# Banded attention and a feed-forward layer on one core: one search's list of steps for another's, and a common order for the transfers of two engines

## The chip, the cores and the metric

The kernel runs on one core of a Trainium2 chip. The metric is the device time of one execution in microseconds (us); the figure to compare is the median over the timed runs. In the profile, PE is TensorE (matmuls), DVE is VectorE, ACT is ScalarE, POOL is GpSimd and SP is SyncE; "ACTq" and "SPq" are DMA transfers that ACT and SP issue. L1243 is line 1243 of the kernel before.

## The reference

```python
def _attn_ref(q, k, v):                      # (8, 8, 576, 64) each
    scores = scale * np.matmul(q, k.transpose(0, 1, 3, 2))
    mask = (rel >= 0) & (rel < window)       # window 64
    scores = np.where(mask, scores, -1000000000.0)
    scores = scores - np.max(scores, axis=-1, keepdims=True)
    attn = np.exp(scores)
    attn = attn / (np.sum(attn, axis=-1, keepdims=True) + 1e-09)
    return np.matmul(attn, v)
def _moe_ref(x, w_in, w_out):                # x (4608, 512), w_in (512, 2048)
    h = x @ w_in
    g = np.maximum(0.01 * h, h)
    return g @ w_out
```

The attention's output, with the heads side by side, is the feed-forward layer's x. All arrays are float32.

## The kernel before

**Stages.** The 4608 tokens go through the feed-forward layer in nine chunks of 512. Weights and activations are split into a high and a low part, and each product of a weight tile and an activation tile is three matmuls of 128 x 128 by 128 x 512 (high by high, high by low, low by high). The first three chunks are multiplied directly: the steps W of the opening and then `early_first` (h, L1038) and `early_second` (acc, L1047). The other six chunks are taken as three pairs with a seven-product scheme: `product` (m, L1243) for x @ w_in, `seventh` (z, L1309) for g @ w_out. Around a product ACT does `put` (L1249) and `leaky` (L1255) and DVE does `add` (L1252); around `seventh` ACT does `wide_high` (L1286) and DVE `wide_low` (L1290) and `combine` (L1293). The sums of weights that this scheme needs are prepared from weights kept in DRAM: ACT issues `fetch` (L1149) and, when the sum is made, `keep` (L1162 and L1165); POOL issues `fill` (L1227), which brings them back.

**Attention between the products.** There are 36 pairs of attention blocks. Pair m needs `load_qk(m)` (a 512 KB transfer issued by ACT, L262), `scores_of(m)` on PE (s, L369), the mask on DVE (L755) or, for some pairs, `copy_of` on ACT (L761), `max_of` on POOL, `minus_of` on DVE (L777), `exp_of` on ACT (L781), `add_of` on POOL, a few small transfers issued by SP, `values_of(m)` on PE (o, L829) and `product_of` on DVE (L854). So PE alternates between groups of feed-forward matmuls and these short visits, called S(m) and V(m) here.

**The order.** Every engine works off its own instructions in the order in which the kernel is written. That order is a list. In the kernel before, it is in two parts: ORDER holds 514 named steps of the opening (raw0, S0, W3, ...), run one after the other; then `op`, `load` and `bulk` collect 2303 numbered steps with what each comes after, and `arrange` runs them in the order of the list PLACES. The end of the file (L1514) chains each engine's instructions in issue order.

**Transfers and semaphores.** Apart from POOL's 84, the program has 475 transfers, 291 of SP and 184 of ACT. The framework gives each of these one of eight semaphores (LANES = 8) in turn, in the order in which its scheduler sees them. A transfer that has the semaphore of an earlier one is issued when that one has landed; until then its engine stands, with all that is listed behind it. In the program before, the turn of SP's and ACT's transfers is that of the scheduler, and 191 of the 475 have another place in it than in the written order, by up to 17 places.

**Steps by number.** The steps that are spoken of below: 818 is S(23), 843 is S(24), 841 is `load_qk(24)`, 820 is `copy_of(23, 0)`, 1285 is a `put` after the product 1284, 800 is `exp_of(22, 0)`, 1213 and 1214 are two `keep` and 1215 and 1216 two `fetch`; 793 is S(22) with `load_qk(22)` as 791, 492 a leaky ACT step after the product step 487, 778 `copy_of(21, 0)` and 766 `exp_of(20, 0)`; 1104 is S(35) with `load_qk(35)` as 1102, 1737 a `put` and 1063 `exp_of(33, 0)`; 961 is V(26), 1411 an `add`, 1425 and 1429 `wide_low`, 924 and 927 `minus_of(27, ...)`, 1461 a `combine`, 914 `product_of(24)`. At the end 2290, 2296 and 2300 are the last `seventh` steps, 2291, 2297 and 2301 the last three additions on DVE (`add_part`, L1329), and 2292 (of 2291), 2298 (of 2297) and 2302 (of 2301) send these results (`send_part`, L1332); 2270 sends an earlier one.

Of the kernel before, what the change touches and what calls it, by code (L numbers as in the profile page):

```python
# [61 lines left out]
PLACES = """  # L62
# [134 lines left out]
def band_attention_ffn(ctx: ExitStack, tc: tile.TileContext, qk, vW, vL, w_in, w_out, eye_mask, out, outT):  # L197
# [415 lines left out]
    def step(name):  # L613
        kind = name.rstrip("0123456789")
        return partial(acts[kind], int(name[len(kind) :]))

    order, late = ORDER.split("|")
    for name in order.split():
        step(name)()
    prev = jobs[-1]  # L620


    plan = []

# [951 lines left out]
```

## Time and profile before

| what | value |
|---|---|
| timed runs | 838.98, 838.88 and 843.11 us; median 838.98 us |
| profiled execution | span 841.2 us, 2.2 us above that median |
| PE busy | 829.1 us of it (99%), 6733 matmuls |
| DVE, POOL, ACT busy | 630.8, 381.5, 369.7 us |
| DMA | 225.75 MB, mean 268 GB/s |

The span of the profiled execution is from the first to the last instruction or transfer of its trace, and the page shows no time around it. PE is close to always busy; what can be read for a change of order are the few places where it is not, and how near the others are to becoming such places. The views used are the table of windows (busy time of each engine in a stretch), the waits (idle time of an engine by the instruction that it waited before and by what released it), timelines, and the chain of work that ended last.

### The profile page before, as it was taken

The page shows a single profiled execution, that of the slowest core. Times are in us where ns is not written, and L with a number is a line of the kernel's source. Part 1 is how long each engine was busy: PE and PEld are TensorE (multiplying, and loading weights), DVE is VectorE, ACT ScalarE, POOL GpSimd, SP SyncE. Part 2 cuts the span into 40 slices and gives each one's busy share as a digit, 9 for nine tenths or more (in the row PEclk, how much of TensorE's full clock was granted, in tenths as well). Part 3 has the DMA queues.
Part 4 walks back from the last instruction along what each step waited for, and adds up shares of the span by engine and source line. Part 5 has one row for each costly group of instructions (what it writes and reads, how often), then busy time and mean ns, then how long its engine had stood idle before and what let it go on. Part 6 is the DMA issues. An engine that isn't in the chain of part 4 may idle for free.

```text
span 841.2 us, 16743 instructions
## 1 busy us (share of the span) xinstructions
PE 829.1 (99%) x6733; PEld 678.1 (81%) x6733; DVE 630.8 (75%) x912; ACT 369.7 (44%) x599; POOL 381.5 (45%) x216
## 2 busy tenths in 40 slices
PE   8999999999999999989999999999999999999997
PEld 5777888888888888868888888887888888888886
DVE  6999897777766698667888987559799863366773
ACT  4666555344423355243564442233545422325432
POOL 5332000897867747687672116797941111111110
PEclk9999999999999999999999999999999999999999
DMA  9886866987887899999999798899998996677772
GB/s 327 278 276 209 310 223 225 319 287 259 277 295 251 271 342 379 365 299 359 361 321 308 224 316 251 255 282 241 261 278 243 317 257 184 190 197 200 212 200 89
DMA packets 131005, 225.75 MB, mean 268 GB/s; under 512 B 15856, under 2 KB 53744, under 8 KB 130928
## 3 DMA queue, kind: packets, MB, share of 16 engines
q0 software_dynamic: 53568, 88.09, 38.8%
q10 hardware_dynamic: 36608, 78.26, 27.6%
q1 hardware_dynamic: 40752, 58.34, 21.7%
q8 instruction: 53, 0.87, 0.4%
q14 instruction: 24, 0.20, 0.1%
HBM read 167.28 MB, written 57.26 MB: 267 GB/s over the span
## 4 chain that ended last, share of the span: by engine, by line
PE 89%; DMA 5%; DVE 3%; issue 1%; ACT 1%; POOL 0%; DVEq 0%; ACTq 0%
PE z L1309 27%; PE m L1243 25%; PE acc L1047 11%; PE h L1038 11%; PE acc L558 4%; PE s L369 4%; PE h L522 4%; PE o L829 3%; DMA w_sums<-pspare 2%; DMA qk<-qk 1%; DMA raw<-w_in 1%; DMA raw<-w_out 1%; DMA w_single<-w 1%; PE o L458 0%; DVE raw L321 0%
## 5 line engine op out<-in xcount | busy, mean ns | idle before, releaser
L1243 PE MATMUL m<-pfew,p 128*128 128x512 f32 x720 | 171.6, 394 | 3.0 <-ACT pxa L1249 2.5
L1243 PEld LDWEIGHTS m<-pfew,p 128*128 128x128 f32 x720 | 135.5, 189 | 32.5 <-ACT pxa L1249 2.9
L1309 PE MATMUL z<-gs,p 128*128 128x512 f32 (+1 forms) x360 | 86.0, 387 | 0.0
L1047 PE MATMUL acc<-p,gs 128*128 128x512 f32 x324 | 80.7, 393 | 0.0
L1309 PE MATMUL z<-pxa,p 128*128 128x512 f32 x324 | 78.5, 391 | 0.0
L1309 PEld LDWEIGHTS z<-gs,p 128*128 128x128 f32 x360 | 67.3, 188 | 13.9
L1309 PE MATMUL z<-pspare,p 128*128 128x512 f32 x324 | 78.0, 389 | 0.0
L1252 DVE TENSOR_TENSOR pxa<-m,pxa 128x512 f32<-128x512 f32 x60 | 41.2, 688 | 48.5 <-PE m L1243 43.6
L770 POOL PARTITION_ALL_REDUCE g<-late_f x20 | 36.3, 1842 | 86.6 <-DVE late_f L755 71.5
L1227 POOL DMA_DIRECT2D p<-w_first x42 | 31.7, 755 | 93.7 <-PE m L1243 51.6
L1309 PEld LDWEIGHTS z<-pspare,p 128*128 128x128 f32 x324 | 60.7, 188 | 12.6
L1309 PEld LDWEIGHTS z<-pxa,p 128*128 128x128 f32 x324 | 60.5, 188 | 12.9 <-issue 0.2
L1243 PE MATMUL m<-pxb,p 128*128 128x512 f32 x288 | 70.6, 391 | 0.0
L1047 PEld LDWEIGHTS acc<-p,gs 128*128 128x128 f32 x324 | 60.0, 188 | 12.8
L773 POOL PARTITION_ALL_REDUCE late_o<-late_f x20 | 65.2, 3274 | 9.6 <-ACT late_f L781 7.4
L773 POOL PARTITION_ALL_REDUCE late_o<-e x18 | 61.5, 3432 | 16.6 <-issue 7.9
L1252 DVE TENSOR_TENSOR p<-m,pxa 128x512 f32<-128x512 f32 x60 | 40.7, 687 | 36.6 <-PE m L1243 35.9
L773 POOL PARTITION_ALL_REDUCE late_o<-late_e x18 | 59.3, 3321 | 10.6 <-ACT late_e L781 6.0
L1243 PEld LDWEIGHTS m<-pxb,p 128*128 128x128 f32 x288 | 53.8, 188 | 11.4
L1227 POOL DMA_DIRECT2D p<-w_sums x24 | 18.0, 749 | 93.1 <-PE z L1309 76.8
L1038 PE MATMUL h<-pxa,p 128*128 128x512 f32 x228 | 55.9, 392 | 0.0
L1038 PEld LDWEIGHTS h<-pxa,p 128*128 128x128 f32 x228 | 42.4, 188 | 9.0
(201 smaller groups left out, 1600.5 us busy)
## 6 DMA issues: line engine op xcount, KB each, us to landing
p<-w_first POOLq DMA_DIRECT2D x42, 1024.0 KB, 7.0
p<-w_sums POOLq DMA_DIRECT2D x24, 1024.0 KB, 6.7
p<-w_second POOLq DMA_DIRECT2D x18, 1024.0 KB, 6.9
qk<-qk ACTq DMA_DIRECT2D x26, 512.0 KB, 6.2
w_single<-w ACTq DMA_DIRECT2D x32, 256.0 KB, 3.7
raw<-w_out ACTq DMA_DIRECT2D x15, 512.0 KB, 4.5
raw<-w_in ACTq DMA_DIRECT2D x14, 512.0 KB, 4.3
more_v<-vL ACTq DMA_DIRECT2D x14, 512.0 KB, 6.0
```

The costliest lines, as they stand in the source:

```text
L369: nc.tensor.matmul(ps[j][t, c : c + QB], k[i][s, p], q[s, w, p], start=not begun and (not more or (w, p) == (0, 0)), stop=not begun and no ...
L522: nc.tensor.matmul(ps, a[:, k, :], b[:, k, part], start=n == 0, stop=n == len(terms) - 1)
L558: nc.tensor.matmul(acc[c, i], a[:, ts], b, start=begin and n == 0, stop=end and n == 2)
L770: nc.gpsimd.partition_all_reduce(most_of(j), e_of(m)[:, j], P, ReduceOp.max)
L773: nc.gpsimd.partition_all_reduce(sum_of(j), e_of(m)[:, j], P, ReduceOp.add)
L829: nc.tensor.matmul(ps[64 * j : 64 * j + 64, c : c + QB], v[:, 2 * p + j], e_of(m)[:, j, c : c + QB], start=True, stop=True,)
L1038: nc.tensor.matmul(ps, a[:, k, :], b[:, k], start=i == 0, stop=i == len(terms) - 1)
L1047: nc.tensor.matmul(acc[c, i], a[:, i * P : (i + 1) * P], b, start=begin and k == 0, stop=n in ends and k == 2)
L1227: nc.gpsimd.dma_start(to, of, max_dma_last_dim=2048)
L1243: nc.tensor.matmul(tiles[b], w[:, 256 * i + 128 * kt : 256 * i + 128 * kt + 128], x_part(OF_X[k], j, kt), start=begin and c == 0, stop=c = ...
L1252: nc.vector.tensor_tensor(to(), tiles[b], x(), ALU.add)
L1309: nc.tensor.matmul(tiles[b + i][:, cut], a, x[:, cut], start=begin and f == first and c == 0, stop=f == half - 1 and c == 2, skip_group_ch ...
```

## The change

PLACES and the old ORDER become one list, ORDER, of 2817 words: the same 514 names and the same 2303 numbers, each once, in another order. `arrange` runs a word that is no number as a named step. Names and numbers now overlap a little: ten numbers stand ahead of the last name. No step is added or left out, and no step's own work is changed. The weights that come late have a list of their own with the same words as before, and a counter `turns_late` gives the late steps the buffers that they had. At the end, besides the chain of each engine, each transfer of SP or ACT is made to follow the transfer ahead of it in the list when that is the other engine's. This dependency is one of scheduling alone (no wait is emitted for it), so that the eight semaphores are taken in the written order.

```diff
-PLACES = """
...
-813 1229 838 1278 1230 1307 818 788 789 1279 819 841 820 1284 1217 1219 1287 1280 1285 1316 790 1218 1231 382 823 821 1289 811 803 1288
...
-2279 2268 2276 2282 2271 2269 2272 2277 2283 2270 2246 2280 2285 2286 2281 2287 2288 2289 2290 2293 2291 2294 2295 2296 2299 2297 2300
-2301 2298 2302 2292
...
+ORDER = """
+raw0 X6 S0 k1 q1 E1 E0 X2 raw1 bits0 X1 v0 sign0 P1 k2 Z1 abs0 q3 bits1 P0 S1 E2 sign1 clamp0 Z0 N1 exp1 abs1 join0 q2 N0 clamp1 exp0
...
+1211 482 1168 483 1158 486 765 776 777 381 487 779 752 756 484 1274 1194 485 1227 769 780 492 1228 778 1164 766 791 488 772 1166 489 1215
...
+1266 1217 1231 1268 516 795 1219 382 1220 1270 515 798 1295 518 513 1267 796 1272 517 797 1275 1213 799 1269 1271 813 801 810 1273 802 838
+1218 818 1277 819 821 1276 1279 1284 1307 1278 822 820 1287 1280 800 787 1232 1285 519 789 826 392 827 841 1289 812 811 792 1288 1236 1283
...
+1406 910 920 889 1420 1407 867 1405 1408 1409 1410 906 922 907 1411 1424 1422 1441 1413 865 1394 1423 1425 923 926 1450 1426 927 1427 1428
...
+1640 1697 1054 1736 1749 1732 1738 1072 1741 1087 1737 1044 1743 1745 1063 1102 1082 1774 1761 1739 1716 1742 1066 1045 1773 1047 1747
...
+2282 2277 2283 2285 2280 2269 2281 2271 2287 2244 2288 2286 2289 2290 2293 2294 2295 2272 2296 2246 2299 2300 2297 2301 2291 2302 2270
+2298 2292
...
-ORDER = """
-raw0 k1 X6 S0 q1 E1 X2 Z1 E0 bits0 sign0 Z0 P1 S1 abs0 v0 P0 raw1 clamp0 join0 N1 E3 bits1 exp1 N0 q2 P3 V1 exp0 sign1
...
+LATE_WEIGHTS = """
...
-    order, late = ORDER.split("|")
-    for name in order.split():
-        step(name)()
     prev = jobs[-1]
+    turns_late = counter(len(jobs))
...
     def arrange():
         placed = set()
-        for n in map(int, PLACES.split()):
+        for word in ORDER.split():
+            if not word.isdigit():
+                yield step(word)
+                continue
+            n = int(word)
...
-    last = {}
+    order_of_issue = mybir.DependencyInfo(mybir.DependencyClass.NoSync, mybir.DependencyReason.SCHED_ONLY)
+    issued, transfer = {}, None
     for ins in nc.cur_bb.bb.instructions:
...
+        if type(ins).__name__ == "InstDMACopy" and ins.engine != mybir.EngineType.Pool:
+            if transfer is not None and transfer.engine != ins.engine:
+                tc.add_manual_dep(ins, transfer.name, order_of_issue, reason="order of transfers")
+            transfer = ins
```

## Rows read from the trace of the kernel before

**Rows 1.** The page: busy time by engine, and two DMA issue lines

```profile
PE 829.1 (99%) x6733; PEld 678.1 (81%) x6733; DVE 630.8 (75%) x912; ACT 369.7 (44%) x599; POOL 381.5 (45%) x216
...
p<-w_first POOLq DMA_DIRECT2D x42, 1024.0 KB, 7.0
...
qk<-qk ACTq DMA_DIRECT2D x26, 512.0 KB, 6.2
```

**Rows 2.** Windows: start:end, length, busy of each engine, PEclk, DMA share, GB/s

```profile
0.00:10.00 10.00, 7.97 (x141) 5.54 (x142) 3.41 (x6) 2.63 (x5) 3.11 (x6) 1.00 0.81 285
10.00:60.00 50.00, 47.61 (x686) 36.51 (x685) 46.59 (x107) 32.58 (x63) 21.53 (x11) 1.00 0.89 295
60.00:345.00 285.00, 285.00 (x2570) 233.25 (x2570) 222.98 (x356) 134.98 (x238) 152.60 (x64) 1.00 0.85 283
345.00:367.00 22.00, 19.03 (x218) 15.18 (x219) 13.03 (x19) 6.93 (x12) 15.38 (x9) 0.92 1.00 322
...
836.00:841.20 5.20, 0.92 (x8) 0.71 (x6) 1.12 (x2) 0.00 (x0) 0.00 (x0) 1.00 0.29 101
```

**Rows 3.** Waits of PE: engine, line, releaser: total us, times, longest

```profile
PE m L1243 <- ACT pxa L1249: 2.5, 1, 2.5
PE idle L594 <- DVE p L605: 1.4, 1, 1.4
PE t L484 <- DVE y L477: 1.4, 2, 0.7
...
PE m L1243 <- DVE pxa L1252: 0.5, 1, 0.5
```

**Rows 4.** Timeline of ACT: start, us, instruction, [idle before, releaser]

```profile
358.42 0.34 ACTq L262 DMA_DIRECT2D qk<-qk  x1
358.86 0.58 ACT L761 COPY late_f<-s 128x512 f32<-128x512 f32 x1 [8.46 <-DMA w_sums<-pspare]
359.34 0.59 ACT L1249 COPY pxa<-m 128x512 f32<-128x512 f32 x1
```

**Rows 5.** Timeline of PE, same columns

```profile
359.98 4.60 PE L1243 MATMUL m<-pfew,p 128*128 128x512 f32 x12 [2.49 <-ACT pxa L1249]
...
366.45 0.36 PE L369 MATMUL s<-qk,qk 64*64 64x64 f32 x3 [0.48 <-DMA qk<-qk]
```

**Rows 6.** Chain of waits that ended last: start, us, what

```profile
101.93 2.72 PE acc L558 x12
...
343.71 14.64 DMA w_sums<-pspare
...
358.42 7.89 DMA qk<-qk
```

**Rows 7.** Tile qk, 330 to 370: times from issue to landing

```profile
DMA to landing us min/median/max: 5.9/7.9/10.0
```

**Rows 8.** Groups by line: line, engine, operation, tiles, xcount | busy, mean ns

```profile
L1252 DVE TENSOR_TENSOR p<-m,pxa 128x512 f32<-128x512 f32 x60 | 40.7, 687 | 36.6 <-PE m L1243 35.9
...
L1290 DVE TENSOR_TENSOR pspare<-p,pspare 128x1024 fp32r<-128x1024 f32 x21 | 25.6, 1219 | 5.6 <-ACT pspare L1286 5.6
...
L1293 DVE TENSOR_TENSOR p<-p 128x1024 f32<-128x1024 f32 x21 | 27.9, 1330 | 0.0
...
L1249 ACT COPY pxa<-m 128x512 f32<-128x512 f32 x24 | 14.1, 587 | 62.2 <-PE m L1243 62.2
...
L781 ACT ACTIVATE late_f<-late_f 128x512 f32<-128x512 f32 x20 | 12.4, 628 | 10.5 <-DVE late_f L777 8.9 <-DVE p L1252 1.5
...
L777 DVE TENSOR_TENSOR late_f<-s,g 128x512 f32<-128x512 f32 x6 | 4.1, 683 | 1.0 <-POOL g L770 1.0
```

**Rows 9.** Timeline of the end, all engines

```profile
836.24 0.69 DVE L1329 TENSOR_TENSOR qk<-z,qk 128x512 f32<-128x512 f32 x1 [1.38 <-PE z L1309]
836.96 1.35 SPq L1332 DMA_DIRECT2D outT<-qk  x3
837.03 0.42 DVE L1329 TENSOR_TENSOR qk<-z_end,qk 128x256 f32<-128x256 f32 x1
```

More of the change, by code (lines that the diff above doesn't have):

```diff
@@ L60 @@
 )
-PLACES = """
[77 rows of a table removed]
-"""
-ORDER = """
-raw0 k1 X6 S0 q1 E1 X2 Z1 E0 bits0 sign0 Z0 P1 S1 abs0 v0 P0 raw1 clamp0 join0 N1 E3 bits1 exp1 N0 q2 P3 V1 exp0 sign1
-V0 k2 E2 P2 sm0 rec0 S2 sm1 abs1 rec1 chi0 E4 clamp1 N2 q4 rest0 v1 join1 q3 chi1 exp2 y1 y0 rest1 N3 raw2 T0 bits2
-exp3 P4 k3 sub4 V2 raw3 sm2 E5 sign2 H0 V3 abs2 sm3 rec2 P5 rec3 y2 L0 exp4 v2 clamp2 y3 sub5 join2 raw4 S3 X1 T1
-bits3 exp5 H1 V4 E6 V5 chi2 P6 sm4 v3 sign3 L1 sm5 rec4 X2 M0 rec5 y4 k5 y5 rest2 k4 E7 abs3 raw5 clamp3 lk0 bits4
@@ L146 @@
-join3 gh0 T2 gl0 H2 sub6 sign4 L2 abs4 M1 P7 W0 clamp4 exp6 join4 raw6 lk1 v4 S4 sub7 V6 bits5 chi4 exp7 rest4 sm6
-sign5 E8 V7 sm7 rec6 rec7 gh1 y6 chi3 q6 P8 abs5 y7 M2 raw7 gl1 T3 rest3 E9 q5 H3 W1 sub8 lk2 clamp5 exp8 L3 bits6 gh2
-join5 P9 raw8 gl2 chi5 V8 bits7 M3 sign6 rest5 lk3 abs6 gh3 S5 sign7 abs7 M4 clamp6 q7 v5 gl3 W2 join6 lk4 raw9 sub9
-clamp7 M5 bits8 exp9 join7 sign8 gh4 sm8 W3 rec8 E10 y8 chi6 P10 abs8 gl4 clamp8 chi7 rest6 raw10 lk5 sub10 V9 join8
-bits9 gh5 exp10 W4 v6 sm9 sign9 k6 rec9 gl5 M6 y9 T4 V10 chi8 rest8 abs9 raw11 lk6 rest7 bits10 clamp9 M7 gh6 H4 sm10
@@ L151 @@
-sign10 E11 join9 W5 abs10 chi9 rec10 L4 y10 clamp10 bits11 join10 P11 sub11 S6 gl6 raw12 rest9 exp11 sign11 chi10 V11
-E12 raw13 rest10 abs11 lk7 sm11 gh7 rec11 P12 y11 W6 E13 T5 clamp11 bits12 join11 sign12 abs12 H5 raw14 gl7 bits13 k7
-sub12 clamp12 exp12 L5 join12 sign13 M8 chi11 chi12 W7 lk8 P13 rest11 raw15 rest12 sub13 bits14 abs13 S7 clamp13 V12
-sign14 join13 sm12 exp13 rec12 y12 E14 gh8 q9 abs14 M9 gl8 clamp14 v7 V13 W8 P14 raw16 bits15 sub14 join14 sm13 rec13
-lk9 y13 E15 chi14 exp14 chi13 rest14 sign15 T6 rest13 raw17 V14 gh9 P15 sm14 sub15 abs15 clamp15 H6 M10 rec14 gl9
@@ L156 @@
-exp15 y14 k8 join15 L6 bits16 V15 W9 sm15 lk10 sign16 raw18 rec15 chi15 rest15 gh10 y15 T7 gl10 abs16 H7 clamp16
-join16 W10 bits17 L7 M11 raw19 sign17 M12 bits18 abs17 chi16 ev0 clamp17 join17 sign18 raw20 bits19 abs18 lk11 chi17
-sign19 rest16 gh11 clamp18 join18 v8 gl11 bits20 chi18 rest17 raw21 ev1 sign20 lk12 rest18 abs19 clamp19 join19 bits21
-gh12 gl12 M13 W11 raw22 abs20 M14 chi19 lk13 sign21 clamp20 abs21 gh13 W12 join20 gl13 clamp21 raw23 lk14 bits22
-sign22 rest19 chi20 gh14 rest20 M15 W13 abs22 join21 bits23 clamp22 raw24 chi21 sign23 join22 chi22 gl14 M16 raw25 W14
@@ L161 @@
-abs23 rest21 bits24 sign24 lk15 clamp23 abs24 join23 gh15 rest22 gl15 bits25 clamp24 M17 sign25 chi23 raw26 lk16 gh16
-abs25 W15 join24 gl16 M18 chi24 clamp25 raw27 rest23 q8 bits26 sign26 abs26 lk17 join25 chi25 rest24 gh17 clamp26
-join26 gl17 bits27 sign27 raw28 abs27 chi26 W16 rest25 lk18 clamp27 join27 rest26 chi27 gh18 bits28 sign28 gl18 W17
-|
+ORDER = """
+raw0 X6 S0 k1 q1 E1 E0 X2 raw1 bits0 X1 v0 sign0 P1 k2 Z1 abs0 q3 bits1 P0 S1 E2 sign1 clamp0 Z0 N1 exp1 abs1 join0 q2 N0 clamp1 exp0
@@ new lines @@
+join1 raw2 E3 raw3 v1 V1 chi1 V0 k3 sm0 sm1 P2 rec1 P3 y1 S2 N2 chi0 rec0 bits2 E4 exp2 rest0 rest1 y0 N3 V2 raw4 sign2 exp3 sm2 E5 T0
+rec2 V3 abs2 bits3 P4 v2 sub4 sm3 y2 H0 S3 L0 rec3 y3 sign3 clamp2 exp4 T1 P5 V4 H1 sub5 sm4 join2 E6 k4 rec4 L1 P6 v3 X2 exp5 chi2 V5 M0
+y4 raw5 q4 abs3 rest2 lk0 sm5 bits4 rec5 gh0 y5 clamp3 q5 sub6 T2 H2 sign4 M1 gl0 E7 exp6 join3 W0 abs4 v4 L2 clamp4 P7 join4 sub7 lk1
+bits5 raw6 chi4 exp7 rest4 sign5 gh1 V6 gl1 S4 sm6 V7 k5 E8 sm7 P8 rec6 chi3 raw7 rec7 y6 abs5 y7 rest3 M2 E9 T3 bits6 sub8 H3 L3 lk2 gh2
@@ new lines @@
+P9 exp8 clamp5 W1 M3 join5 sign6 bits7 chi5 sign7 V8 raw8 gl2 lk3 abs6 sub9 S5 gh3 rest5 sm8 gl3 M4 abs7 W2 clamp6 W3 clamp7 lk4 join6 gh4
+E10 raw9 chi6 exp9 gl4 join7 rec8 raw10 M5 bits8 lk5 W4 k6 gh5 rest6 P10 y8 V9 sign8 abs8 gl5 sub10 bits9 clamp8 join8 M6 chi7 exp10 sm9
+rec9 y9 rest7 bits10 v5 T4 chi8 sign9 V10 rest8 sm10 W5 raw11 sign10 H4 abs9 clamp9 lk6 E11 M7 join9 rec10 abs10 v6 q6 L4 gh6 raw12 chi9
+P11 q7 y10 gl6 clamp10 sub11 exp11 join10 rest9 S6 bits11 raw13 V11 E12 k7 W6 sign11 sm11 v7 rec11 chi10 lk7 y11 abs11 rest10 clamp11
@@ new lines @@
+join11 bits12 P12 gh7 sign12 raw14 gl7 bits13 T5 M8 chi11 abs12 sub12 exp12 clamp12 H5 join12 E13 raw15 sign13 W7 rest11 L5 S7 chi12 abs13
+bits14 sign14 V12 rest12 P13 clamp13 lk8 abs14 join13 sub13 bits15 sm12 rec12 E14 raw16 y12 gh8 gl8 P14 exp13 M9 sign15 lk9 V13 clamp14
+gh9 join14 abs15 sm13 q9 sub14 E15 exp14 rec13 P15 chi14 W8 y13 chi13 rest14 T6 clamp15 sub15 V14 raw17 bits16 sm14 rec14 gl9 M10 y14
+rest13 join15 sign16 v8 exp15 H6 lk10 V15 chi15 sm15 rec15 y15 W9 gh10 rest15 abs16 L6 T7 raw18 bits17 H7 gl10 clamp16 join16 W10 sign17
@@ new lines @@
+raw19 L7 abs17 clamp17 join17 M11 bits18 chi16 raw20 ev0 sign18 bits19 chi17 sign19 abs18 lk11 abs19 clamp18 gh11 rest16 join18 M12 gl11
+ev1 clamp19 M13 bits20 chi18 lk12 rest17 gh12 gl12 raw21 join19 sign20 W11 lk13 raw22 gh13 abs20 gl13 bits21 sign21 M14 rest18 bits22
+chi19 lk14 abs21 clamp21 clamp20 join20 q8 chi20 raw23 rest20 sign22 abs22 rest19 W12 clamp22 join21 bits23 gh14 gl14 W13 M15 M16 chi21
+W14 join22 sign23 rest21 raw24 chi22 bits24 lk15 gh15 sign24 40 M17 abs23 clamp23 join23 abs24 raw25 rest22 clamp24 chi23 raw26 join24
@@ L165 @@
+gl15 lk16 raw27 gh16 gl16 W15 bits25 sign25 M18 rest23 lk17 chi24 abs25 30 clamp25 join25 bits27 gh17 sign27 bits26 39 gl17 raw28 chi25
+W16 sign26 rest24 abs26 k8 clamp26 join26 bits28 rest25 abs27 clamp27 1 join27 sign28 31 chi26 lk18 41 gh18 W17 5 0 42 gl18 rest26 2 chi27
[77 rows of a table added]
+"""
+LATE_WEIGHTS = """
 abs28 raw29 clamp28 join28 bits29 raw30 sign29 rest27 abs29 bits30 chi28 clamp29 sign30 rest28 abs30 join29 clamp30
@@ L723, in band_attention_ffn @@
     weights_of, raw_of, single_of = {}, {}, {}
-    for name in late.split():
+    for name in LATE_WEIGHTS.split():
         kind = name.rstrip("0123456789")
@@ L735, in band_attention_ffn @@
         }[kind]
-        more = [weights_of.get(n - 2, {}).get("rest")] if kind == "join" else []
-        o[kind] = op(engine, us, step(name), *(o.get(b) for b in before), *more, rank=0.3)
+        room_of = [weights_of.get(n - 2, {}).get("rest")] if kind == "join" else []
+        o[kind] = op(engine, us, step(name), *(o.get(b) for b in before), *room_of, rank=0.3)
     all_in = [weights_of[n][k] for n in (28, 29, 30, 31) for k in ("join", "rest")] + [weights_of[27]["rest"]]
@@ L1024, in band_attention_ffn @@
     ends = {n for n in range(len(walk)) if n + 1 == len(walk) or walk[n][0] != walk[n + 1][0]}
-    pair_at = [pairs_of_g[next(turns) % 2] for _ in walk]
+    pair_at = [pairs_of_g[next(turns_late) % 2] for _ in walk]
     h_of, tiles, stage = {}, {}, {}
@@ L1511, in band_attention_ffn @@
         fn()
-    last = {}
+    order_of_issue = mybir.DependencyInfo(mybir.DependencyClass.NoSync, mybir.DependencyReason.SCHED_ONLY)
+    issued, transfer = {}, None
     for ins in nc.cur_bb.bb.instructions:
-        if ins.engine in last:
+        if ins.engine in issued:
             tc.add_manual_dep(
                 ins,
-                last[ins.engine].name,
+                issued[ins.engine].name,
                 mybir.DependencyInfo(mybir.DependencyClass.NoSync, mybir.DependencyReason.DATA),
@@ L1522, in band_attention_ffn @@
             )
-        last[ins.engine] = ins
+        issued[ins.engine] = ins
+        if type(ins).__name__ == "InstDMACopy" and ins.engine != mybir.EngineType.Pool:
+            if transfer is not None and transfer.engine != ins.engine:
+                tc.add_manual_dep(ins, transfer.name, order_of_issue, reason="order of transfers")
+            transfer = ins
 def windows():
```

144 rows, old and new, of tables (ORDER, PLACES) are left out of this document.

## The prediction

> **What bounds the kernel now.** I read the page first: PE is busy for 829.1 of 841.2 us and no other engine for more than 631 [rows 1]. So the only time that an order of steps can give back is PE's idle time, about 12 us, and whatever PE loses while it is busy. The table of windows says where that is [rows 2]: 2.03 us in the first 10 us, 2.39 in the next 50, none from 60 to 345, 2.97 from 345 to 367, and 4.28 after the last matmuls, from 836 on. The rest is full but for half a us. The table of PE's waits then gives names to them [rows 3]: in the opening PE waits for DVE (idle and t, 2.8 us together), at 360 for ACT's L1249 (2.5), at 579 for DVE's L1252 (0.5).
>
> The wait at 360 is the one to follow backwards. In ACT's timeline [rows 4] `load_qk(24)` is issued at 358.42, and behind it stand `copy_of(23, 0)` (358.86, idle for 8.46 us before it, released by a transfer w_sums<-pspare) and `put` 1285 (359.34). PE takes up the product after that `put` at 359.98, 2.49 us late, and its 12 matmuls take 4.60 us [rows 5], where 12 took 2.72 us elsewhere [rows 6]: they ran at the lower of the two levels of the clock, 1.2 GHz, after PE had stood idle; the granted clock of 345 to 367 is 0.92 [rows 2]. The load then lands late as well, and S(24) starts 0.48 us late [rows 5]. The chain of waits has the cause at its head [rows 6]: the transfer w_sums<-pspare of step 1213 was issued at 343.71 and landed 14.64 us later, and `load_qk(24)`, which depends on it for no data, has its semaphore. Price of the whole: 2.49 + (4.60 - 2.72 = 1.88) + 0.48 = 4.85 us.
>
> **The change part by part.** PE's own order changes hardly at all: there are as many attention visits, side by side as often as before. What moves is what ACT, DVE, SP and POOL do between them. I went through the new list visit by visit and added up, for each, the work listed ahead of what it needs, against the PE work listed in the same stretch. The terms, in us:
>
> 1. The stall at 360: -4.85. In the new order of transfers the eighth ahead of 841 is step 382, a store of SP that is listed over 40 words earlier, and 1213 and its like stand ahead of it by far more; 11 transfers stand in that stretch instead of 16. The bound above is 0 (it stays, or comes back in another place: a rival).
>
> 2. In its place, S(24). Before, nine half groups of products (1.36 us each, half of 2.72 [rows 6]) stood between the load and the visit, 12.2 us. Now the load stands behind `put` 1285, which waits for product 1284, and five stand between that and the visit: 6.8 us. The chain is the put 0.59 [rows 8], 0.1 to issue, and the landing, 5.9 / 7.9 / 10.0 us at least / median / most in this stretch [rows 7] and 6.2 over the whole run [rows 1]. That makes 6.6 / 8.6 / 10.7, so PE waits 0 / 1.8 / 3.9. I take 0.8, between what 6.2 and 7.9 give, since the stretch has fewer transfers than before.
>
> The row on the DMA engines speaks for the long landing: their share of this stretch is 1.00 [rows 2]. The Trainium skill (DMA: Bandwidth & Descriptors, section "Issuing engines are not separate DMA queues") has it that transfers of ScalarE, SyncE and GpSimd run on the same 16 engines and interleave, so that an order among them brings no bandwidth; by that the landing would stay at 7.9, the term would be 1.8 and the sum 1.0 higher.
>
> 3. S(35): its load 1102 now stands behind a put and an exponential. 0.59 + 0.63 [rows 8] + 6.0 to 6.5 to land, against 6.8 of products: +0.5 (0 to 0.9).
>
> 4. V(26): DVE has ahead of what it needs an addition, a wide_low, two `minus_of`, another wide_low, a combine and the product of pair 24: 0.69 + 1.22 + 2 x 0.68 + 1.22 + 1.33 + 0.68 = 6.5 [rows 8] (the last taken as a `minus_of`, of the same shape), up to 7.5 if the longest of these take half as long again, against 6.5 of PE work: +0.5 (0 to 0.9).
>
> 5. S(8), near 139: six ACT steps of 0.59 to 0.63 [rows 8] with 0.1 between stand ahead of what it reads, 4.2 against 4.1 of PE work: +0.2 (0 to 1.2, the upper end if ACT waits for one of them).
>
> 6. S(22): its load 791 stands behind a leaky step, a copy and an exponential, 2.0 with their gaps, in a stretch of 10.9 us; with 6.2 or 7.9 to land there is no wait, with 10.0 it is 1.2: +0.2 (0 to 1.2).
>
> 7. The end. Before, the additions ended at 837.45 and SP issued its three transfers from 836.96 in 1.35 us [rows 9], 0.45 each, to 838.31; the span ended 2.9 later. Now the 0.69 addition 2291 stands behind 2301, and 2302, 2270, 2298, 2292 are issued in this order: from 837.45 at 0.45 each the fourth is issued by 839.25 (its data is there at 838.1). That is 0.94 later, and 256 KB more are under way: +1.0 (0.4 to 1.6).
>
> 8. The opening. From 10 to 60 us DVE is busy 46.59 and PE 47.61 of 50 [rows 2]; there the chain swings between them, and the named words have another order. The DVE work is the same in all, the amount listed ahead of PE's next step differs by some tenths either way: +0.3. Below, it can give back no more than the 2.4 that PE is idle; above I take 1.4, one wait such as "idle" more [rows 3].
>
> 9. The wait at 579 (0.5) stays at 0: the add it waits for stands as late as before. POOL's `fill`s come in swapped pairs at a few places; 10.9 us of products stand between the later of such two and its use, against 7.0 to land [rows 1], so they cost nothing; with that cover gone each us of it would be one of PE. The rest of the list I cost at nothing, because windows outside the opening, 345 to 367 and the end show PE busy all of the time [rows 2]: other engines' work there is hidden, with slack that a swap of neighbours doesn't use up.
>
> Sum: -4.85 + 0.8 + 0.5 + 0.5 + 0.2 + 0.2 + 1.0 + 0.3 = -1.35; 841.2 - 1.35 = 839.85, rounded to 839.9. The profiled execution is 2.2 above the median of the runs, 838.98. If the ordinary runs of before have the stall in part or not at all, the gain on them is smaller, and they would go up by as much as 3.5; if they lack 2.2 us somewhere else, the new kernel's would be near 837.7. I can't tell the two apart from one trace, and leave the forecast where its own sum puts it.
>
> **The rivals.**
>
> *A load that comes too late (slower).* Place: S(24). If `load_qk(24)` takes 10.0 us to land, PE waits 3.9 instead of 0.8, and the matmuls after the wait run at the lower clock as they did at 360, 1.88 more: 839.9 + 3.1 + 1.9 = 844.9. It decides from a wait of 2.3 us on, which with the clock's loss is past 843.2; the landing is then 8.4 us or more. For it: the longest landing in the stretch [rows 7]. Against it: the page's figure for all 26 such loads is 6.2 [rows 1]. 0.13.
>
> *A new stall elsewhere (slower).* The semaphores are still eight; a slow transfer (14.64 us [rows 6]) could hold up another one than 841 in the new order. One such costs about what this one did: 839.9 + 4.85 = 844.8. 0.08.
>
> *The stall only changes its place (no change).* The page "DMA: Bandwidth & Descriptors" of the Trainium skill, section "Rules for kernel authors", asks for a semaphore of its own for a DMA; here they stay shared. As a mechanism of this kernel, ACT still stands when the eighth transfer ahead hasn't landed; part of the 4.85 comes back, the small terms are less than feared, and the time is 841 +- 1. 0.16.
>
> *All of it gone (faster).* Terms 2 to 6 all at zero, the end at +0.4 and the opening's 2.4 us given back: 841.2 - 4.85 - 2.4 + 0.4 = 834.4. For it: each of these terms has zero as its lower bound. Against it: five zeros at once, and an opening in which DVE is busy 93% of the time [rows 2]. 0.13.
>
> **How the numbers follow.** A measurement tells this kernel from an unchanged one from about 0.5% on, here 834.8 and 843.2. The forecast, 839.9, has 0.50, and with the case of no change that makes 0.66 for "same"; faster 0.13; slower 0.13 + 0.08 = 0.21. The forecast's own range is 837.5 to 842.2 (terms 2 to 8 half way to their bounds). The range for 8 in 10 reaches from 835.2 to 844.4, into the two outer cases.
>
> **What the new profile would show.** Right: no idle time of ACT of several us behind `load_qk(24)`; PE's waits without L1249 near 360 and with a wait of under 2 us before S(24), S(35) or V(26); granted clock 1.00 from 345 to 367; four transfers of SP at the end and a span that ends 4.5 to 5.5 us after the last matmul. Wrong: a PE wait of over 2 us in any place, or an opening whose PE idle time from 10 to 60 us is under 1 or over 4.

## The result, and the profile after

The new kernel takes 847.56 us (median of 5 runs, 846.78 to 848.64), the kernel before 840.01 us beside it (5 runs, 838.88 to 843.11). The ratio is 1.0088, with a 95% interval of 1.0061 to 1.0115: slower by 0.9%, where 839.9 us and no change were forecast.

Two things have to be set apart in reading it. Each run comes with its span, and the time is some 1.8 us more than the span (847.43 us with a span of 845.7). And the kernel before has a wide spread: in the 58 later runs of it beside the experiments, 836.77 to 844.32 us. The profiled execution from which the prediction was made, with a span of 841.2, so a time of about 843.0, is one of its long ones: it lies 4 us above the median of 838.98, not 2.2, which compared a span with a time. The forecast of 839.9 is a span as well; as a time it is about 841.6.

The windows of the new kernel, with the columns of [rows 2] (its line numbers are two to four lower than those of before):

```profile
0.00:10.00 10.00, 7.84 (x142) 5.42 (x143) 3.88 (x6) 3.12 (x5) 3.75 (x6) 1.00 0.80 291
10.00:60.00 50.00, 47.17 (x687) 37.03 (x686) 48.47 (x109) 32.49 (x63) 20.52 (x12) 1.00 0.87 294
60.00:319.00 259.00, 259.00 (x2338) 211.63 (x2337) 203.50 (x316) 119.26 (x212) 135.51 (x55) 1.00 0.83 280
319.00:345.00 26.00, 22.08 (x202) 16.88 (x201) 21.29 (x33) 11.82 (x22) 13.49 (x8) 0.87 0.99 332
345.00:367.00 22.00, 22.00 (x214) 18.07 (x212) 17.71 (x24) 8.98 (x16) 18.92 (x11) 1.00 0.91 291
367.00:560.00 193.00, 191.90 (x1584) 156.82 (x1584) 151.39 (x201) 80.43 (x123) 108.19 (x66) 1.00 1.02 299
560.00:836.00 276.00, 276.00 (x1556) 228.20 (x1555) 189.04 (x225) 112.59 (x161) 80.71 (x63) 1.00 0.79 225
836.00:845.70 9.70, 4.28 (x25) 3.60 (x23) 1.72 (x3) 0.00 (x0) 0.00 (x0) 0.92 0.23 82
```

The loss at 345 to 367 is gone: PE is busy for all 22 us and the granted clock is 1.00, where [rows 2] have 19.03 and 0.92. A new one stands at 319 to 345: 3.92 us of idle time, and a granted clock of 0.87. A part of that low clock falls into the wait itself, where it costs nothing; the narrower windows show what PE ran at 1.2 GHz after it:

```profile
334.00:337.00 3.00, 0.00 (x0) 0.00 (x0) 2.96 (x5) 0.57 (x2) 2.05 (x1) 0.77 0.84 282
337.00:340.40 3.40, 3.35 (x11) 2.22 (x13) 3.40 (x8) 2.96 (x7) 0.00 (x0) 0.50 0.84 261
340.40:346.00 5.60, 5.60 (x81) 4.87 (x81) 4.45 (x8) 2.43 (x5) 0.00 (x0) 0.82 0.76 271
```

That is 0.50 x 3.4 + 0.18 x 5.6 = 2.7 us more. The opening has 4.99 us of idle time in 60 where it had 4.42. Another 1.1 are idle between 367 and 560. PE's waits in the new kernel, with the columns of [rows 3]:

```profile
PE acc L1045 <- DVE gs L1056: 3.3, 1, 3.3
PE idle L590 <- DVE p L601: 1.4, 1, 1.4
PE o L454 <- ACT p L438: 1.1, 1, 1.1
```

The first line is the new stall: PE waits 3.3 us for a low part that DVE makes (L1056, `low_of`). The chain of work that ended last says what made DVE late (start, us, what):

```profile
324.70 0.53 DVE gs L1056
325.23 8.10 DMA p<-x_rows
333.33 0.02 issue
333.35 1.99 DVE p L991
...
335.71 0.68 DVE e L775
336.39 0.61 DVE gs L1056
337.00 0.04 issue
337.05 3.35 PE acc L1045 x7
```

DVE's own timeline at that place:

```profile
329.97 1.21 DVE L1156 TENSOR_TENSOR pspare<-pspare 128x1024 fp32r<-128x1024 f32 x1
333.35 2.44 DVE L991 TENSOR_TENSOR p<-p 128x256 f32<-128x256 f32 x2 [2.17 <-DMA p<-x_rows]
335.71 0.68 DVE L775 TENSOR_TENSOR e<-s,g 128x512 f32<-128x512 f32 x1
336.31 0.68 DVE L1056 TENSOR_TENSOR gs<-h,gs 128x512 fp32r<-128x512 f32 x1
```

The transfer p<-x_rows is step 1174, the reload of two blocks of x that the next products need. It lands at 333.33. In the new list the two subtractions that read it (1175 and 1177, L991) stand ahead of the low part 494, and so does a `minus_of` (785). DVE idles 2.17 us at the first of them, which then takes 1.99 us, and 494 starts at 336.31; PE stood from 333.80 (337.05 - 3.25). In the old list 494 stands ahead of all three, and in the profile of before the subtractions follow the low part:

```profile
332.89 0.69 DVE L1058 TENSOR_TENSOR gs<-h,gs 128x512 fp32r<-128x512 f32 x1 [0.69 <-ACT gs L1055]
333.50 1.67 DVE L993 TENSOR_TENSOR p<-p 128x256 f32<-128x256 f32 x4
```

The lower clock is not part of every run of the new kernel. The profiled one has a mean granted clock of 0.995; the run of 847.56 us has 0.999, which with its rounding leaves a loss of at most 1.3 us in a span of 845.8 (0.0015 x 845.8) to a lower clock anywhere, and it took as long. No trace of that run was kept, so where it lost its time is not shown.

The end, all engines:

```profile
839.60 0.69 DVE L1327 TENSOR_TENSOR qk<-z,qk 128x512 f32<-128x512 f32 x1 [5.20 <-PE z L1307]
840.40 0.42 DVE L1327 TENSOR_TENSOR qk<-z_end,qk 128x256 f32<-128x256 f32 x1
840.74 0.68 DVE L1327 TENSOR_TENSOR qk<-z,qk 128x512 f32<-128x512 f32 x1
840.85 0.33 SPq L1330 DMA_DIRECT2D outT<-qk  x1
841.23 0.43 SPq L1344 DMA_DIRECT2D outT<-late_o  x1
841.71 0.93 SPq L1330 DMA_DIRECT2D outT<-qk  x2
```

Four sends instead of three stand behind the last additions, and the last is issued at 842.64, where it was 838.31 with a last matmul 3.36 us earlier [rows 9].

### The profile page after: what moved, and what is told of

Same layout as the page of the kernel before. It is cut to its first block, busy times and chain, and to the rows that moved or that the text cites. A ratio compares the mean times of both kernels' runs of the same rounds, so it can differ in the third digit from the quotient of the medians.

```text
span 845.7 us, 16711 instructions
## 1 busy us (share of the span) xinstructions
PE 830.3 (98%) x6733; PEld 677.7 (80%) x6733; DVE 637.0 (75%) x912; ACT 368.7 (44%) x599; POOL 381.1 (45%) x216
## 4 chain that ended last, share of the span: by engine, by line
PE 84%; DVE 6%; DMA 5%; issue 2%; ACT 1%; POOL 0%; SPq 0%; ACTq 0%; DVEq 0%; POOLq 0%
PE m L1241 25%; PE z L1307 22%; PE acc L1045 9%; PE h L1036 9%; PE h L518 5%; PE acc L554 5%; PE s L365 4%; PE o L827 3%; DMA p<-w_first 1%; DVE p L1291 1%; PE o L454 1%; DMA w_sums<-pspare 1%; DMA p<-x_rows 1%; DMA raw<-w_out 1%; DMA x_rows<-late_n 1%
## 5 line engine op out<-in xcount | busy, mean ns | idle before, releaser
L1241 PE MATMUL m<-pfew,p 128*128 128x512 f32 x720 | 168.9, 391 | 0.0
L1045 PE MATMUL acc<-p,gs 128*128 128x512 f32 x324 | 82.6, 400 | 3.3 <-DVE gs L1056 3.3
L771 POOL PARTITION_ALL_REDUCE late_o<-late_f x20 | 65.6, 3300 | 22.2 <-ACT late_f L779 13.8
L771 POOL PARTITION_ALL_REDUCE late_o<-e x18 | 59.3, 3323 | 16.5 <-DMA w_first<-p 5.6
L1241 PEld LDWEIGHTS m<-pxb,p 128*128 128x128 f32 x288 | 53.5, 188 | 12.8 <-issue 0.8
```

The costliest lines, as they stand in the source:

```text
L771: nc.gpsimd.partition_all_reduce(sum_of(j), e_of(m)[:, j], P, ReduceOp.add)
L1045: nc.tensor.matmul(acc[c, i], a[:, i * P : (i + 1) * P], b, start=begin and k == 0, stop=n in ends and k == 2)
L1241: nc.tensor.matmul(tiles[b], w[:, 256 * i + 128 * kt : 256 * i + 128 * kt + 128], x_part(OF_X[k], j, kt), start=begin and c == 0, stop=c = ...
```

## The experiments

To compare executions whose waits lie in different places, I use PE's delay: the start of a step on PE minus the PE work listed ahead of it, each step's work taken from the trace of before. A wait and a lower clock both add to it. The table gives it, in us, against a quiet execution of before (span 836.5, the third group below), at the times at which that execution passes the same steps; the last column is the whole difference of the spans. Each row is one execution.

| profiled execution | at 47 | 319 | 337 | 363 | 442 | 575 | 832 | span |
|---|---|---|---|---|---|---|---|---|
| before, as in the rows above | 0.1 | 0.8 | 0.8 | 4.8 | 4.8 | 4.8 | 4.7 | 4.7 |
| after | 0.3 | 0.6 | 7.7 | 6.7 | 7.3 | 8.4 | 8.1 | 9.2 |
| e1, two subtractions behind the low part | 2.1 | 3.3 | 6.4 | 5.9 | 6.6 | 9.2 | 8.8 | 9.9 |
| e2, fetches behind the high part | 0.8 | 2.1 | 7.6 | 6.7 | 9.4 | 11.7 | 12.9 | 14.0 |
| e5, new list mended | 1.9 | 2.8 | 3.8 | 4.4 | 6.4 | 9.2 | 8.8 | 8.8 |
| e4, new list, scheduler's semaphores | 1.4 | 7.5 | 13.8 | 12.8 | 14.6 | 15.7 | 15.3 | 17.2 |
| e3, old list, written order of semaphores | 3.9 | 4.0 | 4.4 | 8.9 | 9.9 | 9.9 | 9.7 | 10.3 |
| e6, old list, keeps later | 0.1 | -0.2 | -0.2 | 3.4 | 4.8 | 4.8 | 4.6 | 4.6 |
| f1, old list, keeps earlier | 0.5 | 1.4 | 1.4 | 1.8 | 3.0 | 3.0 | 2.8 | 2.8 |
| f4, old list, one keep earlier | 0.2 | 1.0 | 2.2 | 2.4 | 2.4 | 2.4 | 2.2 | 2.1 |

**The new stall: DVE's order or ACT's wait.** ACT, too, stands for 5.4 us ahead of the high part that the low part needs:

```profile
332.42 0.59 ACT L1053 CAST gs<-h 128x512 fp32r<-128x512 f32 x1 [5.42 <-DMA w_sums<-p]
```

Two kernels tell the two apart. e1:

```diff
-1165 1212 1175 1177 1286 496 784 1216 785 497 493 494 782
+1165 1212 1286 496 784 1216 785 497 493 494 1175 1177 782
```

> The new kernel, with two of DVE's steps, 1175 and 1177 (two subtractions of quarters of x that wait for a reload of x from DRAM), moved in the list from ahead of 494 (the low part of a hidden activation, which PE waits for) to right behind it. In the new kernel's profile PE is idle for 3.25 us at 334 to 337, where the low part is made at 336.3, and the granted clock of 330 to 345 is 0.77, which costs about 3.4 us more. Theory A, the order in DVE's queue is the cause: the low part is made at about 333.1, as soon as ACT has given its high part at 333.0, PE's wait shrinks to under 0.5 us, the clock stays up, and the time falls from 847.6 to 840.5 to 842. Rival B, ACT's wait for a transfer (5.4 us before its high part) is the cause: PE still stands for 2 us or more and the time stays at 846 to 848.

Measured: 845.97 us (7 runs, 843.31 to 849.93; ratio to before 1.0068, 1.0043 to 1.0093). In the table the stretch from 319 to 337 costs 3.1 us instead of 7.1. DVE's timeline there:

```profile
332.60 1.21 DVE L1156 TENSOR_TENSOR pspare<-pspare 128x1024 fp32r<-128x1024 f32 x1
335.49 0.69 DVE L775 TENSOR_TENSOR e<-s,g 128x512 f32<-128x512 f32 x1 [1.68 <-POOL g L768]
336.10 0.68 DVE L1056 TENSOR_TENSOR gs<-h,gs 128x512 fp32r<-128x512 f32 x1
336.69 1.72 DVE L991 TENSOR_TENSOR p<-p 128x256 f32<-128x256 f32 x2
```

The low part is no longer behind the reload, but behind the `minus_of` (785), which waits for POOL; PE's waits for low parts there are 0.47 and 0.58 us, and the stretch keeps a granted clock of 1.00. Theory A holds for the stall's larger part, but its time, 840.5 to 842, was missed, and the intervals of the ratios of e1 and of the new kernel overlap, so that the gain in time itself is not clear of noise. In the profiled execution, one of the longer ones (848.24 us), 2.7 us more were lost ahead of 319, with a list that is the same up to there.

e2 moves ACT's two fetches and leaves DVE alone:

```diff
-488 772 1166 489 1215 1174 490 ... 784 1216 785 ... 500 501 1167 786
+488 772 1166 489 1174 490 ... 784 785 ... 500 501 1215 1216 1167 786
```

> The new kernel, with two of ACT's transfers, the fetches 1215 and 1216, moved in the list to behind the leaky step 501, so that ACT does not stand for 5.4 us ahead of the high part 493. Theory A (DVE's queue is the cause): ACT's high part is made at about 327.5, the low part still at 336, PE's wait stays at 2.5 to 3.5 us and the time at 846 to 848.5. Rival B (ACT's wait is the cause): the wait goes and the time falls to 840.5 to 842.

Measured: 849.53 us (6 runs, 845.82 to 852.26; ratio 1.0101, 1.0074 to 1.0129), a little above both forecasts, with 5.5 us lost from 319 to 337 and a PE wait of 2.8 us for the same low part. The high part is now made early, and DVE still waits for the reload:

```profile
329.05 0.59 ACT L1053 CAST gs<-h 128x512 fp32r<-128x512 f32 x1 [0.67 <-PE acc L1045]
```

```profile
335.18 1.46 DVE L991 TENSOR_TENSOR p<-p 128x256 f32<-128x256 f32 x2 [3.15 <-DMA p<-x_rows]
```

ACT's wait is not the cause. PE's delay grows by another 6 us from 363 to the end; that the later fetches bring this is not shown.

**How much of it is order on DVE and ACT.** e5 mends all that I could see in the stretch, and gives the end its old order:

```diff
-479 768 475 1170 476
+479 475 1170 476 768
-1212 1175 1177 1286 496 784 1216 785 497 493 494 782 770 1178 498 499 500 501 1167 786 1179 1176 504 1214 505 1180 771 783 506 758 1171 502 1169 503
+1212 1286 496 784 1216 497 493 494 785 782 770 498 499 500 501 1167 786 502 503 1175 1177 1178 1179 1176 504 1214 505 1180 771 783 506 758 1171 1169
-2290 2293 2294 2295 2272 2296 2246 2299 2300 2297 2301 2291 2302 2270 2298 2292
+2290 2293 2291 2270 2294 2295 2272 2296 2246 2299 2297 2300 2301 2298 2302 2292
```

> The new list with DVE's and ACT's order around S(22) mended and the end as in the old list: low part 476 ahead of 768; low part 494 ahead of 785, 1175 and 1177; high and low part 502 and 503 ahead of 1175; the additions and sends of the end in the old order (2291 ahead of 2297, 2270 early, three sends behind the last addition). Theory A (the new list is slow because DVE makes the low parts that PE needs late, behind steps that wait for reloads and for POOL): the 7 us lost between 319 and 345 fall to 1.5 or less, the end from 5.4 to 4.3 us after the last matmul, and the time to 839.5 to 841.5. Rival (the small waits only move to the next place, because the stretch is bound by DVE's work or by the transfers themselves): 3 us or more are still lost from 319 to 345, and the time is 843 to 846.

Measured: 844.41 us (6 runs, 844.24 to 847.08; ratio 1.0063, 1.0042 to 1.0085). The window of the stretch, and the end:

```profile
319.00:345.00 26.00, 24.10 (x222) 18.98 (x221) 23.51 (x38) 14.50 (x26) 15.56 (x8) 1.00 1.05 341
```

```profile
841.05 1.35 SPq L1330 DMA_DIRECT2D outT<-qk  x3
841.12 0.42 DVE L1327 TENSOR_TENSOR qk<-z_end,qk 128x256 f32<-128x256 f32 x1
```

From 319 to 337 1.0 us is lost instead of 7.1, and the span ends 4.3 us after the last matmul (841.01), no longer 5.4. So the order on DVE is shown as the cause of the stall in the profile, and the order of the last additions and sends as that of the longer end. In time it is another matter: 844.41 us is in the rival's range of 843 to 846 and outside theory A's. The new kernel is 7.6 us above before, e5 5.0 above the runs of before beside it; mending the stall and the end took some 2.5 us off the distance of the medians, and the intervals of the two ratios overlap. The profiled execution, the longest of the six (847.08), loses the rest in waits of 0.2 to 1.5 us: in the opening, 1.3 at the first product of a pair, before two `seventh` steps at 447 and 456, and 1.5 in all for POOL's `fill`s at 400, 518 and 552. No run takes these out one by one, so what makes the remaining 5 us stays open; that the waits only move to the next place is not ruled out.

**List or semaphores.** e4 is the new list without the new dependency (the `if type(ins)...` lines at the end left out), e3 the old list with it:

> The new kernel with the new list, without the dependency between SP's and ACT's transfers, so that the scheduler's own order decides the semaphores again. If the list is what makes the new kernel slow, the stall at 334 stays (DVE's queue is the same) and the time is 846 to 849. If the new order of semaphores is what makes it slow, the time falls to 840 to 843.

> The kernel before with its own list, and the new order of transfers alone (the dependency between SP's and ACT's transfers at the end of the file). The load for pair 24 then has the semaphore of fetch 1216, which landed at 350.5 in the profile of before, no longer that of 1213, which landed at 358.4. If the stall at 360 (4.85 us in that profile) is in every run, the time falls to 834 to 836.5. If it is in a part of the runs only, which the spread of before (838.9 to 843.1) allows, the time is 837 to 839.5 with less spread. If the order of semaphores does harm elsewhere, it is above 841.

e4: 855.25 us (6 runs, 854.29 to 855.68; ratio 1.0169, 1.0145 to 1.0192). e3: 844.21 us (12 runs, 840.77 to 850.26; ratio 1.0059, 1.0031 to 1.0087). Both forecasts of e4 were missed, the list's 846 to 849 and the semaphores' 840 to 843; of e3, the one of harm elsewhere (above 841) came true. So each list is slower with the order of semaphores that it didn't come with: the new one by some 8 us, the old one by 5. In e4, 6 us of it are lost between 47 and 319, where the new kernel loses 0.3. The two halves of the change can't be costed one by one and added: alone they cost 16 and 5 us against before, together 7.6. e3 also missed in its mechanism. The load for pair 24 was issued at 353.74, 4.7 us earlier than in [rows 6], and landed 3.3 us later, at 369.62 instead of 366.31; PE waited 4.65 us for it:

```profile
353.74 15.88 DMA qk<-qk
...
369.75 2.10 PE s L369 x62
```

15.88 us where it had been 7.89. Being issued early is not enough, then, but why it took so long is open: the two keeps were issued at 347.36 and 352.25 and still under way, and in the quiet execution of before the load, issued at 353.46 with one of them still under way, took 8.09. In the opening the load v2 now has the semaphore of an ACT transfer that lands at 18.96, and is issued at 19.01; before it went at 13.64:

```profile
12.22 0.33 SPq L259 DMA_DIRECT2D p<-qk  x1
19.01 0.55 SPq L266 DMA_DIRECT2D v<-vW  x1
```

V4 then waits 2.8 us, most of the 3.9 that the table shows at 47.

**The stall of before.** e7 is the kernel before once more.

> The kernel before itself, one more profiled execution. If the stall at 360 belongs to a part of its executions, this one has, with a chance of two in three, a span of 836 to 838 and PE busy all of the time from 345 to 367; if it belongs to all, the span has the 4.85 us in it whatever its length.

It took 838.27 us, with a span of 836.5. The window, and the chain at the same place:

```profile
345.00:367.00 22.00, 21.07 (x265) 17.43 (x264) 17.23 (x23) 8.54 (x15) 19.50 (x10) 1.00 1.13 369
```

```profile
342.90 10.49 DMA w_sums<-pspare
...
353.46 8.09 DMA qk<-qk
...
361.68 1.28 PE s L369 x64
```

This is the chain of [rows 6], step for step, except that the keep 1213 lands after 10.49 us and not 14.64. It gives its semaphore back as PE passes S(23), and PE waits 0.93 before S(24), nothing else. So the 4.85 us are the price of a keep that was 4 us slower in one execution, and not a part of every run. In how many of the 58 it occurs is not known.

e6 moves the keeps behind the load (`-1273 1213 392`, `-799 1214 800`, `+841 1213 1214 820`):

> The kernel before with one move in its list: the transfers 1213 and 1214 (two keeps of 512 KB that nothing needs soon) stand behind the load for pair 24, no longer ahead of it. The load's semaphore is then that of fetch 1215 (landed at 352.7 in the profile of before), and no transfer of 512 KB is issued by ACT just ahead of it. Theory (a slow keep ahead of the load makes the stall at 360, in the slow part of the runs of before): the load is issued at about 354 and lands by 362, no wait of PE at 360, and the runs of before above 841 disappear: median 837.5 to 838.5. Rival (all transfers in 345 to 367 are slow, because the DMA engines are full, whatever their order): the load still takes 12 us or more, S(24) waits, and the time is 839 to 842, as before.

842.03 us (12 runs, 838.28 to 842.95; ratio 1.0014, 0.9995 to 1.0033). The theory's median, 837.5 to 838.5, was missed. The load landed in 5.7 us and S(24) had no wait, but the stall came back at the next product: the fetch 1235 writes the buffer that the keeps read, and stood behind them on ACT.

```profile
353.86 10.85 DMA w_sums<-pspare
...
364.78 0.33 ACTq L1149
...
365.16 0.64 ACT p L1255
```

f1 moves both keeps the other way (`+775 1213 1214`), f4 one of them (`+816 1213`):

> The kernel before with the two keeps 1213 and 1214 moved the other way, to an earlier place (right behind the load 775, some 8 us ahead of where they stood; their data is made at 319.6). The load for pair 24 then has the semaphore of fetch 1216 (landed at 347.5 in the quiet execution of before), and the fetch 1235, which needs the keeps landed, gets them 8 us sooner. Theory (the stall of before in its slow executions is a keep that lands 10 to 15 us after its issue, against a margin of 0.3 us; earlier, the margin is 6 us): no PE wait from 345 to 372, no execution above 840, median 837.5 to 838.5. Rival (with 1 MB more in flight from 335 to 345, another transfer is late in its place, the loads for pair 23 or S(22) first): the median stays at 839 to 842.

> The kernel before with keep 1213 alone moved earlier, to right behind the load for pair 23 (5 us ahead), and 1214 where it was. The load for pair 24 then has the semaphore of a 4 KB transfer that landed at 349. Theory as for the run with both keeps: no PE wait behind the load for pair 24, median 837.5 to 838.8, but with 1214 landing up to 360 in a slow execution, the fetch 1235 may still be late and a few executions lie above 841. Rival: as before, 839 to 842.

f1: 841.50 us (12 runs, 838.77 to 844.79; ratio 1.0021, 1.0000 to 1.0042). f4: 839.83 us (12 runs, 838.01 to 841.61; ratio 0.9997, 0.9981 to 1.0014). Both theories forecast a median of 838.8 or less, and both were missed. In f1 the rival came true: PE waited 0.84 us for the load of pair 23, and 0.89 before a product at 418, which no one had named. f4 has no execution above 841.61, where 13 of the 58 of before are; its median is the same, and twelve executions are too few to call the difference shown. None of the versions beats the kernel before.

A last kernel had the new list with the old order of its named words. Some of the ten numbers among the last names then stand ahead of steps that they should follow (W17), so part of the output is computed from older contents of buffers.

> The new kernel with the named words in the order that they had in the old list, and all numbers where the new list has them; the transfers still take the semaphores in the written order. If the new opening is what costs, the time falls by 0.5 to 1. If the old opening suffers from the written order of semaphores, as in the old list with that order (v2 then waits for chi0 to land and V4 for v2), PE loses some 3 us near 25 and the time is 849 to 851. If neither, it is 847 to 848.5.

852.36 us (6 runs, 850.32 to 858.27; ratio 1.0164, 1.0130 to 1.0198). The forecast's three cases were all missed. PE was 0.9 us late at 47, not 3, and lost 2.4 at W17, so it says little of the opening; it settles nothing.

## Why the prediction was wrong

- **The step that failed is part 9**, "The rest of the list I cost at nothing". It took the fullness of PE in the old order as slack for any swap. The stretch around S(22) had been looked at for its load alone (part 6). In the profiled execution the order of three DVE steps there cost 7.1 us of PE's delay, 3.3 of it one wait and about 2.7 the lower clock after it; e5, with that order mended, loses 1.0. A PE wait of over 2 us was the prediction's own sign of being wrong. That is not all that part 9 hid: e5 is still 5.0 us above before, and the cause of these stays open.
- **Also in part 9, POOL's `fill`s.** I set 10.9 us of products against the 7.0 to land of [rows 1]. In the new kernel one of them took 11.15 us to land and PE waited 0.4 for it; in e5 such waits add up to 1.5.
- **Part 1: right as a mechanism, mis-sized as a difference.** The stall at 360 went, and PE's delay from 337 to 363 fell by 1.0 where it had grown by 4.0. But the quiet execution of before has no such stall. The prediction said that ordinary runs without it "would go up by as much as 3.5" and then kept to the profiled execution. Against the quiet one its own terms, 0.8 + 0.5 + 0.5 + 0.2 + 0.2 + 1.0 + 0.3, give 3.5 us slower, and the measured difference of the spans is 9.2, that of the medians 7.6.
- **Parts 2 to 6** (2.2 us): no PE wait appears at S(24), S(35), V(26) or S(8), and S(22) was late for another reason. For S(24) the load stood where part 2 has it, behind the `put`, and was issued at 360.30; but it landed in 3.6 us, where 6.2 to 7.9 were taken. PE's delay grew by 1.7 us from 363 to 575 all the same; the waits there, before a product, before two `seventh` steps and for a `fill`, are 1.0 us together, and none had a price in the prediction.
- **Part 7, the end:** +1.0 forecast, 5.42 - 4.28 = 1.14 measured, and undone in e5.
- **Part 8, the opening:** +0.3 forecast, 0.57 more idle time in the first 60 us [rows 2]. Executions of one and the same opening differ by 2 us (0.3 and 2.1 in the table), so that the two lie near each other shows nothing.
- **The rivals:** "a new stall elsewhere" came nearest, with 844.8 and a chance of 0.08. Its mechanism was wrong: not a shared semaphore but a data dependency behind which another DVE step queued. Beside its 0.8, part 2 weighed a landing that stays at 7.9 us. It drew that from the Trainium skill (DMA: Bandwidth & Descriptors, "Issuing engines are not separate DMA queues"), by which transfers that ScalarE, SyncE or GpSimd issue run on the same 16 DMA engines and interleave. The load of the new kernel did not take 7.9 us to land but 3.6, with 291 GB/s moved from 345 to 367 where before had 322. The stretch had less traffic, so this does not speak against the page, and no run here tests what it states.
- **Signs that came true:** no idle time of ACT behind `load_qk(24)`, a granted clock of 1.00 from 345 to 367, four transfers at the end, and a span that ends 5.42 us after the last matmul. They belong to parts 1 and 7; the rest of the sum was wrong beside them.

## What to carry to other kernels

On an engine that works in order, look at what each new neighbour waits for, not only at how long it runs: two subtractions that waited for a reload, put ahead of a step that the bottleneck needed, cost 3.3 us of waiting and the lower clock after it in the profiled execution. Mending the largest wait of a profile need not give its price back: here PE's delay in the stretch fell from 7.1 to 1.0 us and the time by some 2.5. Where a profile shows a stall of some us, take a second execution before it is counted as a gain: a transfer that lands in 10 or in 14 us can make the whole of it. A list and the order in which its transfers share semaphores belong together; exchanging one alone cost 5 to 8 us here.

## What the runs showed of the hardware

The same 512 KB transfer, of the same step in the same program, landed in 14.64 us in one execution of before and in 10.49 in another, and the DMA share of that window was 1.00 and 1.13. The subtraction of 128x256 (L991, L993 in the old list) takes 0.4 us as a rule, and took 1.99 at 333.35 in the new kernel; its spread there, in ns:

```profile
L991 DVE TENSOR_TENSOR p<-p x16: 376/417/2465, 276.2 to 338.2; 128x256 f32<-128x256 f32 x16
```

In all eleven executions of the table (its ten rows and the quiet one) an all-reduce of POOL goes with the long ones: of this line's 48 instructions in each, the 38 that no all-reduce overlapped took 0.37 to 0.43 us; of the 10 that one overlapped, four to six took no longer, and the others 0.66 to 2.46. No run moves an all-reduce, so it is not shown that this is the cause.
